# Both projections of eight column-block pairs by seven products, in shared accumulator banks

## The chip, the cores and the metric

One core of a Trainium2 chip. The metric is device time in microseconds of one execution. PE is TensorE (matmuls), PEld its weight loads, DVE is VectorE, ACT is ScalarE, POOL is GpSimd, SP is SyncE, which issues DMAs.

## What is computed

Sparse attention over 8 batches, 8 heads, 576 positions and 64 dimensions, then a bilinear feed-forward network over the 4608 tokens, with weights of 512 x 1536 (twice) and 1536 x 512:

```python
mask_local = (rel >= 0) & (rel < stride)                       # heads 0 to 3, stride 32
mask_strided = (rel >= 0) & (pos[None, :] % stride == pos[:, None] % stride)   # heads 4 to 7
attn = softmax(where(mask, q @ k.T / 8, -1e9)) @ v
x = attn.transpose(0, 2, 1, 3).reshape(4608, 512)
out = ((x @ w_a) * (x @ w_b)) @ w_out
```

All inputs and the output are float32; the products are made in bfloat16 with float32 sums.

## The kernel before

The tokens are cut into nine tiles `t` of 512. A tile has 16 slots: twelve for the projections (one column block `f` of 128 columns of `w_a` and `w_b` each), four for the output product. Attention of the next batch is spread over the slots of each tile by written-out lists (`STEPS`, `LATER`, `IN_Y`), so that PE always has matmuls between the steps of attention. All engines run in the order in which the program issues the instructions; `do(slot, ...)` appends work of DVE, POOL or SP to the end of a slot.

In a plain slot, `ab_mm` (L614) gives PE four matmuls of 512 columns with `w_a` and four with `w_b`, each into an accumulator bank of its own; ACT copies the first to `a_sb` (L644), DVE multiplies it with the second into `pf` (L647). Four banks (three tagged `mm`, one `tp`) rotate, two to a slot. Two more banks (`o`) and another two (`st`) belong to attention.

Tiles 2 to 8 (`FAST_Y`) make the output product by seven products of quarter size in place of eight (`y_plan`, L797; `y_tail`, L821, for the last tile): token halves times column halves, with sums of `pf` parts made beforehand (`fast_s`, L745) and sums of `w_out` parts (`fast_w`). `Y_ORDER` and `TAIL_ORDER` name the order: a digit for the product and a digit for the parity `q` of the tokens. Products 1, 6, 5 and 3 accumulate in one bank (X), 7 and 4 in another (Z), 2 in a third (Y); ACT or DVE reads a bank between two products of it (`y_post`). `y_store` and `store_half` issue the stores.

In tiles 7 and 8, attention is over. There, four of the six pairs of column blocks `g` (blocks 2g and 2g+1) make the projection with `w_a` in the same manner (`a_pair`, L678): fourteen matmuls of 256 columns, while `w_b` stays at eight of 512. One accumulator bank X takes 1, 6, 5 and 3:

```python
plan = {"1": (X, w(0, 0), x(0, 0)), "2": (Y, w(0, 1), x(1, 0)), "3": (X, ws(3), x(1, 1)), "4": (Z, w(1, 1), xs(3)),
        "5": (X, ws(0), xs(0)), "6": (X, ws(1), xs(1)), "7": (Z, ws(2), xs(2))}
```

The sums of `w_a` blocks come from `wsum_make` (L659, on DVE during tile 6, slots 98 to 104), those of `x` from `xsum_make` (L670). They lie in buffers that attention has given up. The matmuls of `w_a` are interleaved with those of `w_b`, so that each bank is read while PE works into another; ACT copies, DVE adds, POOL adds product 7 (L728). The partial sums of `pf` for the output product follow on DVE pair by pair (L755); in the last tile one of the four goes to POOL for three pairs (L753). At the end of a slot that has such added work, POOL copies one element of the slot's result into `pace` (L1054), which keeps POOL's later work from running ahead.

Of the kernel before, what the change touches and what calls it, by code (L numbers as in the profile page):

```python
# [27 lines left out]
FAST_A = {7: (1, 2, 3, 4), 8: (0, 1, 2, 3)}  # L28
# [3 lines left out]
def kernel(  # L32
# [29 lines left out]
    pst = ctx.enter_context(tc.tile_pool(name="pst", bufs=1, space=bass.MemoryType.PSUM))  # L62
# [23 lines left out]
    vs_buf = [const.tile([NP, HL, RS, VW], BF16, name=f"vs{i}") for i in range(2)]  # L86
# [539 lines left out]
    def ffn_ab(t, f, mid, ab=None):  # L626
# [3 lines left out]
        if f // 2 in FAST_A.get(t, ()):  # L630
            if f % 2 == 0:
                pairs[t, f // 2] = a_pair(t, f // 2)
            return next(pairs[t, f // 2])
# [18 lines left out]
    wav = wa_sb.rearrange("p (j c) (g e m) -> p j c g e m", c=2, e=2, m=128)  # L652
    wsum_a = [flat.rearrange("p (c g m) -> p c g m", c=2, g=FG)
              for flat in [vl_buf[0].rearrange("p a b -> p (a b)")[:, 12 * 128 * z:12 * 128 * (z + 1)] for z in range(2)]
              + [t.rearrange("p a b c -> p (a b c)")[:, :12 * 128] for t in qz_pair[0]]]
    xsum = {t: qz_pair[1][t - 7].rearrange("p a b c -> p (a b c)")[:, :8 * HT].rearrange("p (n c m) -> p n c m", n=4, c=2)
            for t in FAST_A}

    def wsum_make(n):  # L659
        w, s_ = (lambda e, j: wav[:, j, :, :, e]), wsum_a  # L660
# [15 lines left out]
    pairs = {}  # L676

    def a_pair(t, g):  # L678

        pf = pfs[t]  # L680
        pool, nm = ((pst, "st"), (psum4["o"], "o"))[g % 2]
        X = pool.tile([128, 2, 512], F32, tag=nm, name="ax")[:, 0, :HT]
        a = ([fsb.tile([128, TTOK], F32, tag="a_sb", name="a_sb") for _ in range(2)] if g % 2 == 0 else
             [t.rearrange("p h n -> p (h n)")[:, :2 * TTOK].bitcast(F32) for t in kT_buf[0]])
        got = {k: psum4[nm].tile([128, TTOK], F32, tag=nm, name="mm")
               for k, nm in zip((1, "Z", "Y", 0), (("mm", "mm", "tp", "mm"), ("tp", "mm", "mm", "mm"))[g % 2])}
        Z, Y = got["Z"][:, :HT], got["Y"][:, :HT]
        p7 = fsb.tile([128, HT], F32, tag="p7", name="p7")
        quarter = lambda e, k: a[e][:, HT * k:HT * (k + 1)]
        w = lambda e, j: (lambda c: wav[:, j, c, g, e])  # L690
        ws = lambda n: (lambda c: wsum_a[n][:, c, g])
        x = lambda j, k: (lambda c: x_part(t, j, k)[:, c])
        xs = lambda n: (lambda c: xsum[t][:, n, c])
        plan = {"1": (X, w(0, 0), x(0, 0)), "2": (Y, w(0, 1), x(1, 0)), "3": (X, ws(3), x(1, 1)), "4": (Z, w(1, 1), xs(3)),
                "5": (X, ws(0), xs(0)), "6": (X, ws(1), xs(1)), "7": (Z, ws(2), xs(2))}

        def P(k):
            bank, lhs, rhs = plan[k]
            for c in range(2):
                nc.tensor.matmul(bank, lhsT=lhs(c), rhs=rhs(c), start=k in "172" and c == 0, stop=c == 1, skip_group_check=True)  # L700

        x0 = TTOK * t % (XR * S)

        def b_mm(e, kks):
            f = 2 * g + e
            for kk in kks:
                nc.tensor.matmul(got[e], lhsT=wb_sb[:, kk, 128 * f:128 * (f + 1)], rhs=xT[:, kk, x0:x0 + TTOK],  # L707
                                 start=kk == 0, stop=kk == KD - 1)

        def mult(e):  # L710
            halves = lambda v_: v_.rearrange("p (a i s) -> p a i s", i=2, s=16)
            nc.vector.tensor_mul(pf[:, 2 * g + e, :].rearrange("p (i a s) -> p a i s", i=2, s=16),
                                 halves(a[e]), halves(got[e]))

        P("1")
        nc.scalar.copy(quarter(0, 0), X)
        b_mm(1, (0, 1, 2))
        P("6")
        nc.scalar.copy(quarter(1, 0), X)
        b_mm(1, (3,))  # L720
        P("7")
        nc.scalar.copy(p7, Z)
        P("2")
        nc.vector.tensor_tensor(quarter(0, 0), Y, quarter(0, 0), op=ALU.add)
        yield None
        P("5")
        nc.scalar.copy(quarter(1, 1), X)
        nc.gpsimd.tensor_tensor(quarter(1, 1), quarter(1, 1), p7, op=ALU.add)  # L728
        if (t, g - 1) in later:
            later.pop((t, g - 1))()  # L730
        b_mm(0, (0, 1))
        P("4")
        nc.vector.tensor_tensor(quarter(1, 0), Z, quarter(1, 0), op=ALU.add)
        P("3")
        nc.scalar.copy(quarter(0, 1), X)
        b_mm(0, (2, 3))
        mult(1)
        mult(0)
        yield pf[:1, 2 * g + 1, :1]

    later = {}
# [52 lines left out]
    Y_ORDER = [(x[0], int(x[1])) for x in "10 11 70 71 60 61 40 41 50 51 20 21 30 31".split()]  # L794
    TAIL_ORDER = [(x[0], int(x[1])) for x in "10 70 60 11 40 50 71 30 61 20 51 41 31 21".split()]

    def y_plan(t):  # L797

        plan, y = products(t), y_bufs()
        bank = {x: mm_bank([128, 2, HN]) for x in "ZXY"}  # L800

# [53 lines left out]
    def ffn_ys(t, j, mid):  # L855
# [46 lines left out]
    with tc.manual_schedule(engines={ENG.PE, ENG.SP, ENG.Pool, ENG.DVE, ENG.Activation}):  # L902
        early = ExitStack()
        open_psum(early, tp=2, sum=1, misc=1, o=2)
# [133 lines left out]
        for g in range(FG):  # L1038
            for n in (2, 0, 1, 3):
                do(16 * (NT - 1) + 2 * g + 1, fast_s, NT - 1, n, slice(g, g + 1))  # L1040
        for t in FAST_Y[:-1]:
# [46 lines left out]
```

## Time and profile before

| | |
|---|---|
| timed runs | 326.77, 327.73, 326.5 us (median 326.77) |
| profiled execution, first to last instruction | 325.7 us |
| PE busy | 319.1 us, 98% |
| DVE, ACT, POOL busy | 258.2, 188.2, 160.6 us |
| granted PE clock, mean | 0.997 |
| tile 7: projections, output product | 262.5 to 282.4, 282.4 to 291.6 us |
| tile 8: projections, output product | 291.6 to 311.8, 311.8 to 321.2 us |
| end | stores land until about 323.8, last instruction 325.7 us |

The profiled execution is known by its span alone; the timed runs lie 0.8 to 2.1 us above it. A row of the timeline or of a group gives the engine, the line of the kernel, the operation, what it writes and reads, and the shapes; x16 means that many instructions merged. A matmul's record includes its drain, so the price of a matmul is the difference between the starts of two rows, not the length of one. A name such as `qz1l` or `vl` in tiles 7 and 8 is an attention buffer that holds sums now.

### The profile page before, as it was taken

To read this page: it belongs to the slowest core of one execution; us is meant where nothing else is said; L and a number is where in the kernel's file an instruction comes from. 1 tells how busy PE (TensorE), PEld (TensorE's weight loads), DVE (VectorE), ACT (ScalarE), POOL (GpSimd) and SP (SyncE) were. 2 spreads that over 40 slices of the span, in tenths; PEclk is the share of its full clock that TensorE was granted. 3 is DMA by queue.
4 is the path that set the end of the run, shared out by engine and by line. 5 is a ranking of instruction groups with operands and counts; after the bars stand their busy time and mean duration, and the time that the engine had idled before them with its cause. 6 is when DMAs were issued, how large, how long until landed. Compare 5 with 4: busy or idle time off the path is not lost.

```text
span 325.7 us, 7440 instructions
## 1 busy us (share of the span) xinstructions
PE 319.1 (98%) x2672; PEld 209.0 (64%) x2672; DVE 258.2 (79%) x559; ACT 188.2 (58%) x328; POOL 160.6 (49%) x289
## 2 busy tenths in 40 slices
PE   8999999999999999999999999999999999999994
PEld 7754555445545577557999895559555966686573
DVE  6766786888878988898889888988999768837852
ACT  6763775468774476447654765467546655335441
POOL 8945936989848534762576338634113013103300
PEclk9999999999999999999999999999999999999998
DMA  9999999899999798999998999899245040004004
GB/s 159 141 203 202 202 187 172 190 170 146 123 218 139 134 99 96 108 202 149 107 112 170 196 102 100 163 187 118 46 99 147 20 129 1 2 0 131 0 3 129
DMA packets 111920, 40.73 MB, mean 125 GB/s; under 512 B 89868, under 2 KB 108940, under 8 KB 111884
## 3 DMA queue, kind: packets, MB, share of 16 engines
q0 software_dynamic: 85968, 19.48, 65.3%
q1 hardware_dynamic: 25772, 20.71, 27.4%
q8 instruction: 21, 0.34, 0.4%
q14 instruction: 15, 0.12, 0.1%
q10 hardware_dynamic: 144, 0.07, 0.1%
HBM read 39.51 MB, written 11.06 MB: 155 GB/s over the span
## 4 chain that ended last, share of the span: by engine, by line
PE 80%; DMA 8%; POOL 7%; DVE 1%; issue 1%; ACT 1%; POOLq 0%
PE mm L623 41%; PE mm L809 17%; PE mm L873 5%; DMA shared<-in_q_dram 4%; DMA vl<-in_v_dram 4%; PE mm L707 4%; PE st L388 4%; PE o L526 2%; PE ax L700 2%; POOL shared L197 2%; PE mm L838 2%; PE mm L700 2%; PE o L466 1%; PE end L838 1%; POOL wo_sb L255 1%
## 5 line engine op out<-in xcount | busy, mean ns | idle before, releaser
L623 PE MATMUL mm<-xT,wb_sb 128*128 128x512 bf16 (+1 forms) x408 | 93.7, 354 | 0.2 <-DMA wb_sb<-in_moe_w_b_dram 0.2
L623 PE MATMUL mm<-xT,wa_sb 128*128 128x512 bf16 (+1 forms) x408 | 93.7, 354 | 0.0
L644 ACT COPY a_sb<-mm 128x512 f32<-128x512 f32 x90 | 52.6, 585 | 53.9 <-PE mm L623 51.8
L623 PEld LDWEIGHTS <-wb_sb 128*128 128x128 bf16 x416 | 40.1, 98 | 37.1 <-DMA wb_sb<-in_moe_w_b_dram 0.9
L1054 POOL CAST pace<-pf 1x1 f32<-1x1 bf16 x83 | 25.3, 305 | 69.8 <-DVE pf L647 51.2
L647 DVE TENSOR_TENSOR pf<-a_sb,mm 128x512 bf16<-128x512 f32 x68 | 46.2, 680 | 9.2 <-PE mm L623 8.1
L623 PEld LDWEIGHTS <-wa_sb 128*128 128x128 bf16 x416 | 37.4, 98 | 24.0
L409 ACT ACTIVATE p<-st 72x576 bf16<-72x576 f32 (+1 forms) x56 | 36.4, 650 | 15.3 <-PE st L388 15.1
L542 DVE TENSOR_TENSOR xT<-o,xr 64x288 bf16<-64x288 f32 x48 | 21.4, 446 | 14.7 <-ACT xr L536 14.4
L809 PEld LDWEIGHTS <-ps 128*128 128x128 bf16 x288 | 28.0, 98 | 3.1
L786 ACT COPY y_sb<-mm 128x512 f32<-128x512 f32 (+1 forms) x28 | 15.5, 555 | 17.9 <-PE mm L809 15.3
L809 PE MATMUL mm<-wf,ps 128*128 128x256 bf16 x216 | 25.5, 273 | 0.0
L535 ACT ACTIVATE xr<-o 64x576 f32<-64x576 f32 x28 | 18.1, 647 | 12.3 <-PE o L526 12.0
L873 PE MATMUL mm<-wo_sb,pf 128*128 128x512 bf16 x96 | 23.4, 379 | 0.1
L243 POOL DMA_DIRECT2D vs<-in_v_dram x24 | 19.6, 818 | 5.1 <-PE mm L809 2.4
L809 PEld LDWEIGHTS <-pf 128*128 128x128 bf16 x216 | 20.3, 98 | 2.5 <-issue 0.2
L1054 POOL COPY pace<-y_sb 1x1 f32<-1x1 f32 x23 | 5.4, 233 | 33.2 <-DVE y_sb L784 19.8
L536 ACT ACTIVATE xr<-xr 64x576 f32<-64x576 f32 x28 | 19.1, 683 | 0.9
L212 POOL DMA_DIRECT2D ql<-in_q_dram x24 | 15.9, 664 | 6.3 <-DMA wo_sb<-in_moe_w_out_dram 4.6
L707 PE MATMUL mm<-xT,wb_sb 128*128 128x512 bf16 x64 | 19.0, 379 | 0.0
L809 PE MATMUL mm<-wo_sb,pf 128*128 128x256 bf16 x144 | 18.5, 273 | 0.1
L649 DVE TENSOR_TENSOR pf<-a_sb,mm 128x512 bf16<-128x512 f32 x22 | 14.9, 676 | 4.7 <-ACT a_sb L644 2.7
(189 smaller groups left out, 566.4 us busy)
## 6 DMA issues: line engine op xcount, KB each, us to landing
out_dram<-y_sb SPq DMA_DIRECT2D x12, 512.0 KB, 5.8
out_dram<-y_sb SPq DMA_DIRECT2D x11, 256.0 KB, 4.1
vl<-in_v_dram POOLq DMA_DIRECT2D x6, 384.0 KB, 8.2
kl<-in_k_dram POOLq DMA_DIRECT2D x24, 72.0 KB, 3.3
ql<-in_q_dram POOLq DMA_DIRECT2D x24, 72.0 KB, 3.2
vs<-in_v_dram POOLq DMA_DIRECT2D x24, 72.0 KB, 4.4
wo_sb<-in_moe_w_out_dram POOLq DMA_DIRECT2D x4, 384.0 KB, 9.3
natk<-in_k_dram POOLq DMA_DIRECT2D x20, 72.0 KB, 3.4
```

The costliest lines, as they stand in the source:

```text
L243: nc.gpsimd.dma_start(out=vs_buf[b % 2][:, h, :, 0:D], in_=v[b, HL + h].rearrange("(p r) d -> p r d", r=RS))
L409: nc.scalar.activation(p_flat(p)[:M, :2 * W].rearrange("p (i n) -> p i n", n=2 * n), st[:M].rearrange("p a (i n) -> p (a i) n", n=256)[:, ...
L535: nc.scalar.activation(r, sums, ACT.Ln)
L536: nc.scalar.activation(r, r, ACT.Exp, scale=-1.0)
L542: nc.vector.tensor_mul(dst.rearrange("d (p r) -> d p r", r=RS)[:, :, G * half:G * (half + 1)], o[:64, j, :W].rearrange("d (g p) -> d p g", ...
L623: nc.tensor.matmul(ps_[:, c0:c0 + n], lhsT=w[:, kk, 128 * f:128 * (f + 1)], rhs=xT[:, kk, x0:x0 + n], start=(kk == first and c0 == 0), sto ...
L644: nc.scalar.copy(a_sb, ab[0])
L647: nc.vector.tensor_mul(pf[:, f, :].rearrange("p (i a s) -> p a i s", i=2, s=16), halves(a_sb), halves(ab[1]))
L707: nc.tensor.matmul(got[e], lhsT=wb_sb[:, kk, 128 * f:128 * (f + 1)], rhs=xT[:, kk, x0:x0 + TTOK], start=kk == 0, stop=kk == KD - 1)
L809: nc.tensor.matmul(bank[b][:, q], lhsT=lhs(g, q), rhs=rhs(g), start=k in "172" and q == 0 and g == 0, stop=g == FG - 1, skip_group_check=True)
L873: nc.tensor.matmul(ybank[j], lhsT=pf[:, f, 128 * j:128 * (j + 1)], rhs=wo_sb[:, f], start=(f == 0), stop=(f == FD - 1))
L1054: nc.gpsimd.tensor_copy(pace, done)
```

## The change

In tiles 7 and 8 all slots of the projections come from one generator, `joint(t)`. A tile is two halves (`JOINT`): in each a plain pair (0, then 5) and two joint pairs (1 and 2, then 3 and 4). A joint pair makes both projections by seven products. Its banks X, Y and Z are 512 wide: `w_a`'s part lies in columns 0 to 255, `w_b`'s in 256 to 511, so one ACT copy or DVE add serves both. `JOINT_ORDER` interleaves, for each half, the products of the two joint pairs (`1a`, `1b`, ...) with the plain blocks (`A0`, `B0`, `A1`, `B1`). The products of the two projections are then multiplied in quarters: three by POOL from SBUF, one by DVE straight from the bank.

All eight banks are shared out anew for this (`eight`): the pools `o` and `st` are closed when tile 7 begins, and their four banks become Za, B, Zb and A; the four rotating banks become Ya, Yb, Xb and Xa. The output products of both tiles use them too.

Moved: the sums of `w_b` blocks are made by POOL in tile 6 (slots 99, 101, 103, 105); `xsum_make` for tile 7 in one go ahead of the tile; the partial sums of `pf` in tiles 7 and 8 no longer slot by slot, but for pairs 0 to 2 in the first eight steps of the second half, and for pairs 3 to 5 behind its last step, all on DVE. `pace` is no longer written in these two tiles. The token order inside `pf` is plain there, and the stores' row patterns follow it. `Y_ORDERS` has a second order for tile 7; `TAIL_ORDER` is new, and with it the places of two stores. Pools are opened in another order at the start, with as many banks.

```diff
-FAST_A = {7: (1, 2, 3, 4), 8: (0, 1, 2, 3)}
+JOINT = {7: ((0, 1, 2), (5, 3, 4)), 8: ((0, 1, 2), (5, 3, 4))}
...
-    vs_buf = [const.tile([NP, HL, RS, VW], BF16, name=f"vs{i}") for i in range(2)]
+    vs_all = [const.tile([128, HL, RS, VW], BF16, name=f"vs{i}") for i in range(2)]
+    vs_buf = [t[:NP] for t in vs_all]
...
+    WS = 2 * FG * 128
+    wsum = [[h.rearrange("p (c g m) -> p c g m", c=2, g=FG) for h in homes] for homes in (
+        [flat(vl_buf[0])[:, WS * z:WS * (z + 1)] for z in range(2)] + [flat(t)[:, :WS] for t in qz_pair[0]],
+        [flat(vs_all[0])[:, WS * z:WS * (z + 1)] for z in range(2)] + [flat(nat_s[nm]) for nm in "qk"])]
...
+    def wsum_make(s, n, eng):
...
         for c in range(2):
-            nc.vector.tensor_tensor(s_[n][:, c], a[:, c], b[:, c], op=op)
+            eng.tensor_tensor(s_[n][:, c], a[:, c], b[:, c], op=op)
...
+    def eight(nm, shape=(128, 2, HT)):
+        if not ends:
+            psums.close()
+            ends["pool"] = ctx.enter_context(tc.tile_pool(name="pend", bufs=1, space=bass.MemoryType.PSUM))
+            for x in ("Za", "B", "Zb", "A"):
+                eight(x)
+        pool, tag = {"Ya": (psum4["mm"], "mm"), "Yb": (psum4["mm"], "mm"), "Xb": (psum4["mm"], "mm"),
+                     "Xa": (psum4["tp"], "tp")}.get(nm, (ends["pool"], f"e{nm}"))
+        return pool.tile(list(shape), F32, tag=tag, name=f"e{nm}")
...
+    JOINT_ORDER = ("1a A0 B0 2a 1b 7a 6a 2b 7b 6b A1 5a 5b B1 4a 3a 4b 3b",
+                   "A0 1a 1b B0 7a 6a 7b 6b A1 2a 5a 2b 5b B1 4a 3a 4b 3b")
...
+                    for s in range(2):
+                        for c in range(2):
...
+                            nc.tensor.matmul(bank[:, s], lhsT=w, rhs=x, start=k in "172" and s == 0 and c == 0, stop=c == 1,
+                                             skip_group_check=True)
...
+                    if k in "176":
+                        nc.scalar.copy({"1": s1, "7": s3, "6": s2}[k], bank)
+                    elif k == "3":
+                        nc.scalar.copy(c12, bank[:, 0])
+                        mult(nc.vector, 0, 1, c12, bank[:, 1])
+                    else:
+                        c, e, kk = {"2": (s1, 0, 0), "5": (s3, 1, 1), "4": (s2, 1, 0)}[k]
+                        nc.vector.tensor_tensor(c, bank, c, op=ALU.add)
+                        mult(nc.gpsimd, e, kk, c[:, 0], c[:, 1])
+                if half and at_ < 8:
+                    fast_s(t, at_ % 4, slice(0, 1) if at_ < 4 else slice(1, 3))
+                if (half, at_) == (1, len(order) - 1):
+                    for n in range(4):
+                        fast_s(t, n, slice(3, 6))
+                if at_ % 3 == 2:
+                    yield None
...
-    Y_ORDER = [(x[0], int(x[1])) for x in "10 11 70 71 60 61 40 41 50 51 20 21 30 31".split()]
-    TAIL_ORDER = [(x[0], int(x[1])) for x in "10 70 60 11 40 50 71 30 61 20 51 41 31 21".split()]
+    Y_ORDERS = [[(x[0], int(x[1])) for x in o.split()] for o in
+                ("10 11 70 71 60 61 40 41 50 51 20 21 30 31", "10 11 20 21 60 61 70 71 50 51 40 41 30 31")]
+    TAIL_ORDER = [(x[0], int(x[1])) for x in "10 11 20 60 70 61 50 71 40 51 30 41 31 21".split()]
...
-                if k == "54"[q]:
+                if k == "4":
                     y_store(nc.sync, t, y, 1, q)
-                elif (q, k) == (0, "2"):
+                elif (q, k) == (0, "3"):
                     y_store(nc.sync, t, y, 0, q)
...
-            do(16 * (NT - 3) + 2 * n + 2, wsum_make, n)
+            do(16 * (NT - 3) + 2 * n + 2, wsum_make, 0, n, nc.vector)
+            do(16 * (NT - 3) + 2 * n + 3, wsum_make, 1, n, nc.gpsimd)
         do(16 * (NT - 2) - 1, xsum_make, NT - 2, 0)
         for n in (2, 1, 3):
-            do(16 * (NT - 2), xsum_make, NT - 2, n)
+            do(16 * (NT - 2) - 1, xsum_make, NT - 2, n)
```

More of the change, by code (lines that the diff above doesn't have):

```diff
@@ L61 @@
     fsb = ctx.enter_context(tc.tile_pool(name="ffn", bufs=2))
-    pst = ctx.enter_context(tc.tile_pool(name="pst", bufs=1, space=bass.MemoryType.PSUM))
+    psums = ctx.enter_context(ExitStack())
     dram = ctx.enter_context(tc.tile_pool(name="dram", bufs=2, space=bass.MemoryType.DRAM))
@@ L380, in S_p @@
         kT = kT_buf[b % 2][c // 2]
-        st = pst.tile([128, 2, 512], F32, tag="st", name="st")
+        st = psum4["st"].tile([128, 2, 512], F32, tag="st", name="st")
         held[b, "st", u] = st
@@ L629, in ffn_ab @@
         pf = pfs[t]
[L630 to L633, printed above, removed]
+        if t in JOINT:
+            if f == 0:
+                joints[t] = joint(t)
+            return next(joints[t])
         if ab is None:
@@ L650, in ffn_ab @@
         return pf[:1, f, :1]
[L652 to L660, printed above, removed]
+    wviews = [w.rearrange("p (j c) (g e m) -> p j c g e m", c=2, e=2, m=128) for w in (wa_sb, wb_sb)]
+    flat = lambda t: t.rearrange({2: "p a -> p a", 3: "p a b -> p (a b)", 4: "p a b c -> p (a b c)"}[len(t.shape)])
+    WS = 2 * FG * 128
+    wsum = [[h.rearrange("p (c g m) -> p c g m", c=2, g=FG) for h in homes] for homes in (
+        [flat(vl_buf[0])[:, WS * z:WS * (z + 1)] for z in range(2)] + [flat(t)[:, :WS] for t in qz_pair[0]],
+        [flat(vs_all[0])[:, WS * z:WS * (z + 1)] for z in range(2)] + [flat(nat_s[nm]) for nm in "qk"])]
+    xsum = {t: flat(qz_pair[1][t - 7])[:, :8 * HT].rearrange("p (n c m) -> p n c m", n=4, c=2) for t in JOINT}
+    def wsum_make(s, n, eng):
+        w, s_ = (lambda e, j: wviews[s][:, j, :, :, e]), wsum[s]
         a, b, op = ((w(1, 0), w(1, 1), ALU.add), (s_[0], w(0, 0), ALU.subtract), (w(0, 0), w(1, 0), ALU.subtract),
@@ L674, in xsum_make @@
         nc.vector.tensor_tensor(s_[:, n], a, b, op=ALU.subtract)
-    pairs = {}
-    def a_pair(t, g):
-        pf = pfs[t]
[L681 to L739, printed above, removed]
@@ L741 @@
-    later = {}
+    joints = {}
+    ends = {}
+    def eight(nm, shape=(128, 2, HT)):
[7 more added lines that the diff above has]
+        return pool.tile(list(shape), F32, tag=tag, name=f"e{nm}")
@@ new lines @@
+    f32 = lambda t, n, i=0: flat(t)[:, 2 * n * i:2 * n * (i + 1)].bitcast(F32)
+    pair_of = lambda t: t.rearrange("p (s m) -> p s m", s=2)
+    held_s = [pair_of(x) for x in [f32(vl_buf[1], TTOK, i) for i in range(3)] + [f32(vs_all[1], TTOK, i) for i in range(4)]
+              + [f32(kT_buf[i][z], TTOK) for i, z in ((0, 0), (0, 1))]]
+    held_c = [f32(p_buf[i], HT) for i in range(3)]
+    JOINT_ORDER = ("1a A0 B0 2a 1b 7a 6a 2b 7b 6b A1 5a 5b B1 4a 3a 4b 3b",
+                   "A0 1a 1b B0 7a 6a 7b 6b A1 2a 5a 2b 5b B1 4a 3a 4b 3b")
@@ new lines, in joint, with mult @@
+    def joint(t):
+        pf = pfs[t]
+        fill = []
+        for half, (plain, *gs) in enumerate(JOINT[t]):
+            banks = {x: eight(x) for x in "Ya Yb Xb Zb Xa Za".split()}
+            order = JOINT_ORDER[half].split()
+            for at_, (k, m) in enumerate(order):
+                if k in "AB":
+                    f = 2 * plain + int(m)
+                    if k == "A":
+                        ab = [eight("A", [128, TTOK]), eight("B", [128, TTOK])]
+                    ab_mm(t, f, ab, range(KD), ws=("AB".index(k),))
+                    if k == "A":
+                        a_sb = fsb.tile([128, TTOK], F32, tag="a_sb", name="a_sb")
+                        nc.scalar.copy(a_sb, ab[0])
+                    else:
+                        nc.vector.tensor_mul(pf[:, f, :], a_sb, ab[1])
+                else:
+                    z = "ab".index(m)
+                    g, (s1, s2, s3), c12 = gs[z], held_s[3 * z:3 * z + 3], held_c[z]
+                    bank, lhs, rhs = {"1": ("X", (0, 0), (0, 0)), "2": ("Y", (0, 1), (1, 0)), "3": ("X", 3, (1, 1)),
+                                      "4": ("Z", (1, 1), 3), "5": ("X", 0, 0), "6": ("X", 1, 1), "7": ("Z", 2, 2)}[k]
+                    bank = banks[bank + m]
+                    for s in range(2):
+                        for c in range(2):
+                            w = wsum[s][lhs][:, c, g] if isinstance(lhs, int) else wviews[s][:, lhs[1], c, g, lhs[0]]
+                            x = xsum[t][:, rhs, c] if isinstance(rhs, int) else x_part(t, *rhs)[:, c]
+                            nc.tensor.matmul(bank[:, s], lhsT=w, rhs=x, start=k in "172" and s == 0 and c == 0, stop=c == 1,
+                                             skip_group_check=True)
+                    def mult(eng, e, kk, a, b):
+                        eng.tensor_tensor(pf[:, 2 * g + e, HT * kk:HT * (kk + 1)], a, b, op=ALU.mult)
+                    if k in "176":
[3 more added lines that the diff above has]
+                        mult(nc.vector, 0, 1, c12, bank[:, 1])
+                    else:
+                        c, e, kk = {"2": (s1, 0, 0), "5": (s3, 1, 1), "4": (s2, 1, 0)}[k]
[8 more added lines that the diff above has]
+                    yield None
@@ L751, in fast_s @@
                     (x[:, 0, 0], x[:, 0, 1], ALU.subtract), (x[:, 1, 0], s[:, 1], ALU.subtract))[n]
-        if (t, n) == (NT - 1, 2) and {gs.start, gs.start + 1} <= set(FAST_A[t]):
-            later[t, gs.start] = lambda: nc.gpsimd.tensor_tensor(s[:, n], a, b, op=op)
-            return
         nc.vector.tensor_tensor(s[:, n], a, b, op=op)
@@ L773, in y_store @@
     def y_store(eng, t, y, i, q, n=slice(0, d_model)):
-        rows = out[TTOK * t:TTOK * (t + 1), n].rearrange("(a i s q) c -> a s i q c", i=2, s=8, q=2)
-        eng.dma_start(out=rows[:, :, i, q], in_=y[i][:, q, n])
+        rows = out[TTOK * t:TTOK * (t + 1), n].rearrange("(i p q) c -> p i q c", i=2, q=2)
+        eng.dma_start(out=rows[:, i, q], in_=y[i][:, q, n])
     def y_bufs():
@@ L792, in y_post @@
             nc.scalar.copy(part(0, 1), bank)
-    Y_ORDER = [(x[0], int(x[1])) for x in "10 11 70 71 60 61 40 41 50 51 20 21 30 31".split()]
-    TAIL_ORDER = [(x[0], int(x[1])) for x in "10 70 60 11 40 50 71 30 61 20 51 41 31 21".split()]
+    Y_ORDERS = [[(x[0], int(x[1])) for x in o.split()] for o in
+                ("10 11 70 71 60 61 40 41 50 51 20 21 30 31", "10 11 20 21 60 61 70 71 50 51 40 41 30 31")]
+    TAIL_ORDER = [(x[0], int(x[1])) for x in "10 11 20 60 70 61 50 71 40 51 30 41 31 21".split()]
     def y_plan(t):
         plan, y = products(t), y_bufs()
-        bank = {x: mm_bank([128, 2, HN]) for x in "ZXY"}
+        bank = ({k: eight(x) for k, x in (("X", "Ya"), ("Z", "Yb"), ("Y", "Xb"))} if t in JOINT else
+                {x: mm_bank([128, 2, HN]) for x in "ZXY"})
         def store_half(i):
-            rows = out[TTOK * t:TTOK * (t + 1)].rearrange("(a i s q) c -> a s i (q c)", i=2, s=8, q=2)
-            nc.sync.dma_start(out=rows[:, :, i], in_=y[i].rearrange("p q c -> p (q c)"))
-        for n, (k, q) in enumerate(Y_ORDER):
+            rows = out[TTOK * t:TTOK * (t + 1)]
+            rows = (rows.rearrange("(i p q) c -> p i (q c)", i=2, q=2)[:, i] if t in JOINT else
+                    rows.rearrange("(a i s q) c -> a s i (q c)", i=2, s=8, q=2)[:, :, i])
+            nc.sync.dma_start(out=rows, in_=y[i].rearrange("p q c -> p (q c)"))
+        for n, (k, q) in enumerate(Y_ORDERS[t in JOINT]):
             b, lhs, rhs = plan[k]
@@ L823, in y_tail @@
         plan, y = products(t), y_bufs()
-        banks = [{x: mm_bank([128, HN]) for x in "ZXY"},
-                 {"X": psum4["o"].tile([128, 2, 512], F32, tag="o", name="end")[:, 0, :HN],
-                  "Z": pst.tile([128, 2, 512], F32, tag="st", name="end")[:, 0, :HN]}]
+        banks = [{x: eight(n)[:, 0] for x, n in zip("XZY", ns)} for ns in (("Ya", "Yb", "Xb"), ("Xa", "Za"))]
         for k, q in TAIL_ORDER:
@@ L833, in y_tail @@
                 if (q, k) == (1, "2"):
-                    bank = mm_bank([128, 128])
+                    bank = eight("A" if n.start == 0 else "B", [128, TTOK])[:, :128]
                 else:
@@ L864, in ffn_ys @@
                 pass
-        return (y[0][:1, 0, :1], None, y[1][:1, 0, HN:HN + 1], y[1][:1, 0, :1])[j]
+        return None if t in JOINT else (y[0][:1, 0, :1], None, y[1][:1, 0, HN:HN + 1], y[1][:1, 0, :1])[j]
     def ffn_y(t, j, mid):
@@ L903 @@
         early = ExitStack()
-        open_psum(early, tp=2, sum=1, misc=1, o=2)
+        open_psum(early, tp=2, sum=1, misc=1, o=2, st=1)
         cur["misc"] = psum4["misc"].tile([128, 512], F32, tag="misc", name="misc")
@@ L963 @@
                     if f == 1:
-                        ab = pst.tile([128, 2, 512], F32, tag="st", name="ab")
+                        ab = psum4["st"].tile([128, 2, 512], F32, tag="st", name="ab")
                         first[f] = [ab[:, 0], ab[:, 1]]
@@ L974 @@
         early.close()
-        open_psum(ctx, mm=3, tp=1, o=1)
+        open_psum(ctx, mm=3, tp=1)
+        open_psum(psums, o=1, st=1)
         slots = []
@@ L992 @@
         soon = {}
-        for t in FAST_Y[:-1]:
+        for t in FAST_Y[:-2]:
             soon[16 * t + 10] = [lambda t=t: fast_s(t, 2, slice(4, 6))]
@@ L1037 @@
             do(slot, fast_w, n, slice(3, 6))
[L1038 to L1041, printed above, removed]
+        for t in FAST_Y[:-2]:
             for slot, n, z0, z1 in ((4, 0, 0, 2), (5, 2, 0, 2), (6, 1, 0, 2), (7, 3, 0, 2), (8, 2, 2, 4), (9, 0, 2, 4),
```

## The prediction

> **What bounds the kernel now.** I read the page first, then the matmul timeline of the last two tiles, then the vector and GpSimd timelines, and last quarter-microsecond windows over the end.
>
> ```profile
> PE 319.1 (98%) x2672; PEld 209.0 (64%) x2672; DVE 258.2 (79%) x559; ACT 188.2 (58%) x328; POOL 160.6 (49%) x289
> ```
>
> TensorE (PE) is busy 98% of the span, at full clock. A change pays only if it shortens the matmul stream, and costs wherever that stream waits. The stream of the last tiles:
>
> ```profile
> 262.49 0.81 PE L623 MATMUL mm<-xT,wa_sb 128*128 128x512 bf16 x3
> ...
> 265.94 0.38 PE L700 MATMUL ax<-xT,wa_sb 128*128 128x256 bf16 x2
> ...
> 278.96 1.03 PE L623 MATMUL mm<-xT,wa_sb 128*128 128x512 bf16 x4
> ...
> 282.42 1.47 PE L809 MATMUL mm<-wo_sb,pf 128*128 128x256 bf16 x12
> ...
> 291.58 0.38 PE L700 MATMUL ax<-xT,wa_sb 128*128 128x256 bf16 x2
> ...
> 311.80 0.82 PE L838 MATMUL mm<-wo_sb,pf 128*128 128x256 bf16 x6
> ```
>
> Differences of starts give prices. Pair 5 of tile 7 (278.96 to 282.42) is 16 matmuls of 512 columns: 0.216 us each. The 84 matmuls of 256 columns from 282.42 to 291.58 cost 0.109 each, each with its own weight load. The four pairs with a fast A (265.94 to 278.96) cost 3.255 each. There is almost no wait to remove; the chain of waits shows one, at the start of tile 8, where PE had to wait for ScalarE (ACT):
>
> ```profile
> 291.79 0.58 ACT y_sb L792
> 292.37 0.28 ACT a_sb L716
> ```
>
> The timeline puts that gap at about 0.09 us.
>
> **The change, part by part.**
>
> *Matmuls.* A fast-A pair is 14 matmuls of 256 and 8 of 512. A joint pair is 28 of 256: 28 x 0.109 = 3.052. Saved: 0.203 a pair, 1.62 us for eight (1.73 if a 256 cost half a 512). All of this is on the path. The wait at the start of tile 8 goes too, since the first joint product is followed by 1.7 us of plain matmuls: 0.09.
>
> *Evacuations inside a half.* A half is 6.10 + 3.46 = 9.56 us of PE. ACT gets seven 512-wide copies (0.585) and two 256-wide (0.37): 4.8 us. DVE (VectorE) gets six adds of 512 and two plain products, 0.605 apart when queued (two L712 rows together last 1.28), and two 256-wide products, 0.34 apart: 5.5 us. In the second half it also gets eight partial sums (0.20 to 0.42 each), 2.8 us. Both fit. Two places are tight. Product 5b of the first half overwrites a bank that ACT reads for 6b: behind 1b, 7a, 6a and 7b that copy ends 0.16 us ahead. Product 1b of the second half needs the bank of the last half's 3b, which DVE leaves some 1.2 us into the half; PE comes to it at 1.3. I cost both at nothing; a DVE or ACT that is later than its rows pays there.
>
> *The hand-over to the output stage.* Count from the start of 2a in the second half. PE ends 2a 0.44, 5a 0.87, 2b 1.31, 5b 1.74, B1 2.61, 4a 3.04, 3a 3.48, 4b 3.92, 3b 4.35; call this T. DVE starts 0.27 behind a matmul's end (311.80 to 312.07 in the timeline), so its queue runs: 2a from 0.71 to 1.31, 5a 1.92, 2b 2.52, 5b 3.13, B1 3.73, 4a 4.34, 3a 4.68, 4b 5.28, 3b 5.62, landed at 5.70 = T+1.35. The output stage's second product wants that same bank at T+1.31. GpSimd's product for 4b lands about T+1.83 (0.73, the L728 row, behind the add), wanted by the fifth matmul of that output product at T+1.75. Together these stall PE about 0.15 us. Four 768-wide sums follow, 0.55 each: the second ends at T+2.53, the third at T+3.0. In tile 7 the first matmul that reads them comes at T+3.1: free. In the last tile the output products are six matmuls long, so it comes at T+2.44: 0.13 more. Stalls: 0.15 for tile 7, 0.28 for tile 8. Bounds: nothing, if a record is longer than the hold of the bank; 0.75 more at each, if nine queued DVE operations take their whole 0.69 and not 0.605. I take the middle, since queued rows are 0.60 apart throughout.
>
> *The last stores.* Of the last tile's stores, the 256 KB of y1, first row, now follow product 40 (ninth of fourteen, before: sixth), and those of y0 follow 30 (eleventh) where they followed 20 (tenth).
>
> ```profile
> 320.25:320.50 0.25, 0.25 (x6) 0.24 (x4) 0.14 (x1) 0.00 (x0) 0.00 (x0) 1.00 0.93 205
> ...
> 321.25:321.50 0.25, 0.00 (x0) 0.00 (x0) 0.25 (x1) 0.00 (x0) 0.00 (x0) 1.00 0.32 115
> ...
> 323.50:323.75 0.25, 0.00 (x0) 0.00 (x0) 0.00 (x0) 0.00 (x0) 0.00 (x0) 0.75 0.65 168
> ```
>
> In these windows (DMA share and GB/s last) a 256 KB store occupies the DMA engines about 1.1 us, 1.2 behind its issue, and the last 512 KB take 2.1 us from 321.6. PE ends at 321.17 = E. After: the first store runs E-1.45 to E-0.35, y0 from E-0.2 to E+0.95, and the last 512 KB, which could have started at E+0.43, start there: 0.5 us later than now. Bounds 0 and 0.6.
>
> *Moved work off the path.* The eight sums of w_b weights go to GpSimd in tile 6, two instructions behind each of slots 99, 101, 103, 105. They are needed at about 265.5. A 128x256 bf16 sum takes 0.67 there (L753) and a one-element operation 0.17 (L1054), so 768 elements are estimated at 0.17 + 3 x 0.50 = 1.67 us, 13.4 in all, from about 238: ready in time even with waits. Behind them GpSimd has only pace operations, on which no load depends any more. What they do to DVE is the rival below. The sums of x for tile 7 move one slot forward, into DVE time that is free at 264.
>
> *Sum.* -1.62 - 0.09 + 0.15 + 0.28 + 0.50 = -0.78. The profiled span of 325.7 becomes 324.9; the median of the runs, 326.77, is 1.1 above that span, and gives 326.0. Own range of this case, from the bounds: 325.0 to 327.6. A measurement can tell about 0.5%, 1.6 us, from no change; this is inside.
>
> **Rivals.**
>
> *GpSimd holds up DVE in tile 6 (slower).* Some DVE operations read two tensors in SBUF (masks, partial sums, weight sums), others one in SBUF and one in PSUM. The first kind and GpSimd get in each other's way:
>
> ```profile
> 243.77 1.57 POOL L1054 CAST pace<-pf 1x1 f32<-1x1 bf16 x1 [1.45 <-DVE pf L647]
> ...
> 271.80 0.74 POOL L728 TENSOR_TENSOR a_sb<-a_sb,p 128x256 f32<-128x256 f32 x1 [1.52 <-ACT a_sb L727]
> ```
>
> The pace operation, 0.17 elsewhere, lasts until DVE's run of a mask, two weight sums and a partial sum (243.57 to 245.30) is over. But the 0.74 at 271.80 began under a DVE sum that ran to 271.96 and is only 0.02 longer than the undisturbed 0.72. No row shows a DVE operation that waits for GpSimd. If it does, for the whole instruction, each of the eight can start only behind a DVE operation of the other kind (0.6 for a plain product, 1.3 where a normalisation follows), so DVE loses 0.4 to 1.07 each time, more where the start comes late in such an operation; I take 0.85: 6.8 us in all. DVE is idle about 1.1 us from 235 to 252, and a plain product may be 1.7 us late before the matmuls two pairs of banks on wait for it: about 4 us reach PE. With half a microsecond of the same at the hand-overs (partial sums behind GpSimd's last product) the time is 330.5. It decides from a DVE loss of 2.8 us, 0.35 an instruction. The Trainium skill, "SBUF — State Buffer", section "Who interferes with whom", has this as a rule: whichever of a two-SBUF-input VectorE operation and a GpSimd operation that reads SBUF starts first keeps the shared ports for its whole length. By that rule this rival is the outcome; the trace agrees in the one direction that the pace row shows.
>
> *DVE later than its rows inside the joint halves (slower).* If DVE and ACT come 0.5 us later than counted, both tight places and the hand-overs wait, about 0.4 us twice in each of four halves and 0.5 at each hand-over: 4.2 on -0.78 would be the worst, half of it likely: 328.1. Against: the four fast-A pairs run with the same kind of hand-offs and no PE gap.
>
> *The whole gain (faster).* If the stores overlap and nothing stalls: 326.77 - 1.82 = 324.95. Against: the stores fill the DMA windows to 0.9 already.
>
> *The products do not come cheaper.* If four different weights in a row were not loaded in time, the gain would be nothing; the 84 matmuls at L809 do just that at 0.109, so I give this no chance of its own.
>
> **How the numbers follow.** Forecast 0.43 (no change that can be told); GpSimd holding DVE 0.42, of it 0.40 slower; late DVE 0.08, 0.05 of it slower; whole gain 0.07. Faster 0.07, same 0.48, slower 0.45. I put the forecast a little ahead of the rival because the one overlapped GpSimd sum hardly noticed DVE. The range must reach over both: 325.0 to 332.0 leaves out part of the whole-gain case and the worst of the rival.
>
> **What would show it.** Right: joint products at 0.436 us each, eight pairs' worth shorter by 1.6 us; the first output matmul of tile 7 about 0.8 us earlier than 282.42, with the gap of 0.1 to 0.2 us behind twelve of them; DMA active to about 3.0 us behind the last matmul. Wrong: PE gaps between 240 and 262 with DVE idle before a mask or a sum while GpSimd runs its weight sums (the rival); gaps before product 1b or 5b (late DVE); w_b sums on GpSimd far from 1.7 us.

## The result, and the profile after

The changed kernel takes 330.67 us (median; 329.82 to 331.63), the kernel before 326.48 beside it (325.92 to 327.73): a ratio of 1.0126, 95% interval 1.0105 to 1.0146. It is slower, by 1.3%. The profiled span went from 325.7 to 329.9.

The first line of the page answers to the one shown of before.

```profile
PE 317.1 (96%) x2691; PEld 212.8 (64%) x2720; DVE 267.3 (81%) x551; ACT 188.7 (57%) x320; POOL 180.2 (55%) x295
```

PE has 2 us less to do, as the change meant, and its share of the span fell. So it waits, and the matmul timeline says where. Behind the name of a group stand the idle time ahead of it and what ended it.

```profile
244.64 1.03 PE L624 MATMUL mm<-xT,wa_sb 128*128 128x512 bf16 x3
246.55 1.02 PE L624 MATMUL mm<-xT,wb_sb 128*128 128x512 bf16 x4 [0.88 <-DVE pf L648]
...
249.76 1.02 PE L624 MATMUL mm<-xT,wb_sb 128*128 128x512 bf16 x4 [1.08 <-DVE pf L648]
...
252.72 1.02 PE L624 MATMUL mm<-xT,wb_sb 128*128 128x512 bf16 x4 [0.81 <-DVE pf L648]
...
255.94 1.02 PE L624 MATMUL mm<-xT,wb_sb 128*128 128x512 bf16 x4 [1.08 <-DVE pf L648]
...
258.72 0.94 PE L818 MATMUL mm<-wo_sb,pf 128*128 128x256 bf16 x7 [0.94 <-DVE pf L648]
...
262.13 1.05 PE L818 MATMUL mm<-wf,ps 128*128 128x256 bf16 x8 [0.47 <-DVE ps L760]
...
268.80 0.38 PE L728 MATMUL eXa<-xT,wa_sb 128*128 128x256 bf16 x2
...
288.11 1.47 PE L818 MATMUL eYa<-wo_sb,pf 128*128 128x256 bf16 x12
...
297.36 0.38 PE L728 MATMUL eXa<-xT,wa_sb 128*128 128x256 bf16 x2
...
316.49 0.82 PE L845 MATMUL eYa<-wo_sb,pf 128*128 128x256 bf16 x6
```

Four plain products and two output products wait for DVE, and all of it is in tile 6, which the joint products do not touch. Tile 7 starts at 268.80; before it was 262.49. Measured from the same early matmuls of tile 6, it starts 6.27 us late. What DVE and GpSimd (POOL) do there is seen in their timelines, GpSimd first:

```profile
238.11 3.23 POOL L666 TENSOR_TENSOR vs<-wb_sb 128x768 bf16<-128x768 bf16 x2
...
243.80 3.72 POOL L666 TENSOR_TENSOR vs<-vs,wb_sb 128x768 bf16<-128x768 bf16 x2
...
249.98 3.73 POOL L666 TENSOR_TENSOR natq<-wb_sb 128x768 bf16<-128x768 bf16 x2
...
256.16 3.41 POOL L666 TENSOR_TENSOR natk<-wb_sb,vs 128x768 bf16<-128x768 bf16 x2
```

```profile
239.73 1.93 DVE L428 TENSOR_TENSOR p<-p,mask_l 128x576 int16<-128x576 int16 x1 [0.17 <-ACT p L410]
...
244.14 1.75 DVE L760 TENSOR_TENSOR ps<-pf 128x512 bf16<-128x512 bf16 x1
245.82 0.67 DVE L648 TENSOR_TENSOR pf<-a_sb,mm 128x512 bf16<-128x512 f32 x1
246.42 1.42 DVE L428 TENSOR_TENSOR p<-p,mask_s 72x576 int16<-72x576 int16 x1
```

A mask takes 0.45 and a partial sum 0.41 when undisturbed. The mask at 239.73 ends at 241.66, 0.32 behind the end of the GpSimd pair (241.34); the mask at 246.42 ends at 247.84, 0.32 behind the next pair. DVE records the operation as busy while it is held. The partial sum at 244.14 does not wait for its whole pair: it ends at 245.89, 0.27 behind the first sum of the pair (1.82 us from 243.80), and the second sum ends only behind it. The plain product between them (L648, one input in PSUM) keeps its 0.67 while GpSimd sums. Seven DVE operations are held so, each by one GpSimd sum, for 1.47, 1.34, 0.96, 1.34, 0.97, 0.91 and 0.74 us, 7.7 in all. The first is absorbed by DVE's lead, the time by which it was ahead of what PE needs; the other six come to 6.26, and the PE gaps, taken from the starts of groups (246.55 - 244.64 less four matmuls of 0.216, and so on), are 1.04, 1.23, 0.97, 1.23, 1.12 and 0.64: 6.23 us.

The rest of the span, stage by stage (starts of the groups above against those of before; the output stages' starts are 282.42 and 311.80 before):

| stretch | before | after | change |
|---|---|---|---|
| up to tile 7 | 262.49 | 268.80 | +6.31 |
| projections of tile 7 | 19.93 | 19.31 | -0.62 |
| output of tile 7 | 9.16 | 9.25 | +0.09 |
| projections of tile 8 | 20.22 | 19.13 | -1.09 |
| output of tile 8 to PE's end | 9.37 | 9.90 | +0.53 |
| PE's end to the span's end | 4.53 | 3.50 | -1.03 |

They sum to +4.2, the difference of the spans. PE ends at 321.17 before and at 326.40 after.

The end of the span, in half-microsecond windows (DMA share and GB/s last):

```profile
326.50:327.00 0.50, 0.00 (x0) 0.00 (x0) 0.22 (x1) 0.00 (x0) 0.00 (x0) 1.00 1.01 373
...
327.50:328.00 0.50, 0.00 (x0) 0.00 (x0) 0.00 (x0) 0.00 (x0) 0.00 (x0) 1.00 1.02 270
328.00:328.50 0.50, 0.00 (x0) 0.00 (x0) 0.00 (x0) 0.00 (x0) 0.00 (x0) 1.00 0.02 5
```

The DMA engines are done about 1.7 us behind PE's end instead of 2.6. Before, a 256 KB store ran at 164 to 205 GB/s in three of its quarter-microsecond windows, with the engines 0.82 to 0.94 busy, and at 369 only in the fourth; here the loaded windows have 270 to 373.

### The profile page after: what moved, and what is told of

Read it like the earlier page. It is cut to its first block, busy times and chain, and to the rows that moved or that the text cites. A ratio compares the mean times of both kernels' runs of the same rounds, so it can differ in the third digit from the quotient of the medians.

```text
span 329.9 us, 7496 instructions
## 1 busy us (share of the span) xinstructions
PE 317.1 (96%) x2691; PEld 212.8 (64%) x2720; DVE 267.3 (81%) x551; ACT 188.7 (57%) x320; POOL 180.2 (55%) x295
## 4 chain that ended last, share of the span: by engine, by line
PE 72%; DMA 8%; DVE 8%; POOL 7%; issue 3%; ACT 1%; POOLq 0%; DVEq 0%
PE mm L624 32%; PE mm L818 13%; PE mm L880 5%; DMA vl<-in_v_dram 4%; DMA shared<-in_q_dram 4%; PE st L389 3%; PE o L527 2%; PE eA L624 2%; PE eXb L728 2%; PE eXa L728 2%; PE eB L624 2%; DVE ps L760 2%; POOL shared L198 2%; PE eYa L818 2%; DVE pf L648 2%
## 5 line engine op out<-in xcount | busy, mean ns | idle before, releaser
L624 PE MATMUL mm<-xT,wb_sb 128*128 128x512 bf16 (+1 forms) x373 | 85.0, 352 | 4.2 <-DVE pf L648 3.9
L624 PE MATMUL mm<-xT,wa_sb 128*128 128x512 bf16 (+1 forms) x360 | 83.9, 351 | 0.7
L645 ACT COPY a_sb<-mm 128x512 f32<-128x512 f32 x82 | 47.9, 585 | 49.0 <-PE mm L624 41.5
L1060 POOL CAST pace<-pf 1x1 f32<-1x1 bf16 x71 | 22.8, 321 | 45.2 <-DVE pf L648 31.8
L648 DVE TENSOR_TENSOR pf<-a_sb,mm 128x512 bf16<-128x512 f32 x60 | 40.7, 679 | 6.4 <-PE mm L624 6.1
L732 POOL TENSOR_TENSOR pf<-vl 128x256 bf16<-128x256 f32 x12 | 8.7, 729 | 30.8 <-DVE vl L741 30.8
L760 DVE TENSOR_TENSOR ps<-pf 128x512 bf16<-128x512 bf16 (+2 forms) x42 | 21.6, 514 | 0.6
L818 PE MATMUL mm<-wf,ps 128*128 128x256 bf16 x180 | 21.5, 273 | 0.5 <-DVE ps L760 0.5
L213 POOL DMA_DIRECT2D kl<-in_k_dram x24 | 16.1, 671 | 5.3 <-issue 3.2
L791 ACT COPY y_sb<-mm 128x512 f32<-128x512 f32 x20 | 11.7, 585 | 12.1 <-PE mm L818 10.5
L650 DVE TENSOR_TENSOR pf<-a_sb,mm 128x512 bf16<-128x512 f32 x22 | 14.9, 677 | 4.5 <-ACT a_sb L645 2.7
```

The costliest lines, as they stand in the source:

```text
L213: nc.gpsimd.dma_start(out=t[32 * h:32 * h + 32], in_=src[b, h].rearrange("(i y) d -> y i d", y=32))
L624: nc.tensor.matmul(ps_[:, c0:c0 + n], lhsT=w[:, kk, 128 * f:128 * (f + 1)], rhs=xT[:, kk, x0:x0 + n], start=(kk == first and c0 == 0), sto ...
L645: nc.scalar.copy(a_sb, ab[0])
L648: nc.vector.tensor_mul(pf[:, f, :].rearrange("p (i a s) -> p a i s", i=2, s=16), halves(a_sb), halves(ab[1]))
L760: nc.vector.tensor_tensor(s[:, n], a, b, op=op)
L818: nc.tensor.matmul(bank[b][:, q], lhsT=lhs(g, q), rhs=rhs(g), start=k in "172" and q == 0 and g == 0, stop=g == FG - 1, skip_group_check=True)
```

## The experiments

Theory: GpSimd's weight sums hold DVE's operations with two inputs in SBUF; the expectations call this the port theory. Rivals: the joint products themselves, the shared banks or the new order are what costs. Ratios are to the kernel before, run beside each, with 95% intervals.

### The changed kernel without the w_b sums

The products that need a w_b sum take w_a's in its place, so the same matmuls run and the output is wrong.

```
-            do(16 * (NT - 3) + 2 * n + 3, wsum_make, 1, n, nc.gpsimd)
-   w = wsum[s][lhs][:, c, g] if ...
+   w = wsum[0][lhs][:, c, g] if ...
```

> The changed kernel without the eight w_b sums on GpSimd; the w_b half of products 3, 5, 6 and 7 takes w_a's sums as weights instead, so the same matmuls run. Port theory (a VectorE operation with two SBUF inputs waits for a whole GpSimd sum): the 6.3 us that tile 7 starts late are gone, 330.7 - 6.3 = 324.4 us, and no mask or partial sum in tile 6 takes over 0.5 us. Rival (the joint halves or their VectorE backlog cost the time): 328 us or more.

Measured: 324.92 us, 0.9951 (0.9932 to 0.9969), span 323.2. Tile 7 starts where it did before, to 0.01 us, counted from the matmuls of tile 6. The projections of tiles 7 and 8 take 19.31 and 19.13 as in the changed kernel, 1.71 us less than before, which is in sum what the forecast gave the joint products and the start of tile 8. The sums on GpSimd are worth 5.8 us.

### The kernel before with the eight sums

```
+    def wsum_make_b(n):
+        ...
+        for c in range(2):
+            nc.gpsimd.tensor_tensor(s_[n][:, c], a[:, c], b[:, c], op=op)
...
+            do(16 * (NT - 3) + 2 * n + 3, wsum_make_b, n)
```

> The kernel before, with the eight w_b sums added on GpSimd at the same slots, read by nobody. Port theory: 326.5 + 6.3 = 332.8 us, with masks and partial sums of 1.3 to 1.9 us in tile 6. Rival (the cost lies in the joint halves): 326.5 us.

Measured: 332.92, 1.0195 (1.0179 to 1.0211), span 331.3: 6.5 us slower than before with nothing but the sums. Tile 7 starts 6.27 us late, the same as in the changed kernel, and the DVE timeline shows the same held rows, the first of them this mask:

```profile
239.04 1.93 DVE L428 TENSOR_TENSOR p<-p,mask_l 128x576 int16<-128x576 int16 x1 [0.17 <-ACT p L410]
```

With the run above this shows the cause from both sides: the sums alone make it slower, and the change without them is faster.

### GpSimd as busy, but only writing

```
+            if eng is nc.gpsimd:
+                for _ in range(2):
+                    eng.memset(s_[n][:, c], 0.0)
+                continue
```

> The changed kernel with each GpSimd sum replaced by two memsets of the same target (estimated 0.7 us each from the 1.40 us of a 1536-element one), so that GpSimd is busy as long but reads nothing; the w_b sums are zero. Port theory, for reads: no wait, 324.4 us as without sums. Rival theory, that any GpSimd work in tile 6 or its writes slow VectorE or shift the queue: 328 to 331 us.

Measured: 324.30, 0.9933 (0.9918 to 0.9948). GpSimd's timeline, then DVE's under it:

```profile
240.87 2.99 POOL L668 MEMSET vs<- 128x768 bf16 x4
```

```profile
242.18 0.45 DVE L428 TENSOR_TENSOR p<-p,mask_s 72x576 int16<-72x576 int16 x1
```

The mask runs inside the 2.99 us in which GpSimd writes, and takes its usual 0.45. GpSimd being busy, or writing, is not what costs: it is its reading.

### One read instead of two

As above, with `eng.tensor_copy(s_[n][:, c], a[:, c])` in place of the memset.

> The changed kernel with each GpSimd sum replaced by two GpSimd copies of one SBUF operand into the same target (w_b sums are then copies of a weight block). Port theory, any GpSimd read of SBUF: 16 instructions of an estimated 0.8 us, masks and partial sums in tile 6 are again longer than 0.46 us, by up to 0.8 each; 326.5 to 329 us. Rival (only a GpSimd operation with two SBUF inputs holds VectorE up): as without sums, 324.4 us.

Measured: 326.49, 1.0004 (0.9995 to 1.0013). Tile 7 starts 2.34 us late; the masks and partial sums of DVE that start under a copy (0.82 undisturbed) take up to 1.20, so none loses more than one copy:

```profile
238.57 1.14 DVE L428 TENSOR_TENSOR p<-p,mask_l 128x576 int16<-128x576 int16 x1 [0.17 <-ACT p L410]
```

One input in SBUF suffices for the hold.

### The same sums in short pieces

```
-            eng.tensor_tensor(s_[n][:, c], a[:, c], b[:, c], op=op)
+            for g in [slice(z, z + 1) for z in range(FG)] if eng is nc.gpsimd else [slice(0, FG)]:
+                eng.tensor_tensor(s_[n][:, c, g], a[:, c, g], b[:, c, g], op=op)
```

> The changed kernel with each of the eight sums cut into six GpSimd instructions of 128 columns (estimated 0.17 + 0.25 = 0.42 us each, 20 us in all). Port theory, held for one instruction: no VectorE operation waits more than 0.42 us, some thirteen runs of two-SBUF operations lose 0.2 each, which VectorE's idle time and the banks' slack absorb; 324.4 to 326 us. Rival (GpSimd keeps the port as long as it has work): 331 us or more.

Measured: 329.92, 1.011 (1.0077 to 1.0142). My expectation missed; the rival put beside it, at 331 or more, came nearer. The four runs lie between 328.42 and 331.88, and the trace is of the slowest. GpSimd's pieces and, from the DVE timeline, what met them, for the first and the last of the four groups:

```profile
238.19 4.64 POOL L667 TENSOR_TENSOR vs<-wb_sb 128x128 bf16<-128x128 bf16 x12
```

```profile
239.81 3.35 DVE L428 TENSOR_TENSOR p<-p,mask_l 128x576 int16<-128x576 int16 x1 [0.17 <-ACT p L410]
...
263.29 3.81 DVE L790 TENSOR_TENSOR y_sb<-y_sb 128x512 f32<-128x512 f32 x1
```

A piece takes 0.39, but the mask, ready at 239.8, ended at 243.2, behind the whole run of twelve. The addition at 263.29 was held behind the last twelve pieces (261.89 to 266.54); the last piece of xT came behind it, and PE stood 2.1 us at the start of tile 7. Behind this stand the granted clock is 0.57 from 268 to 272. In the two groups between, DVE did get in. The third, then a mask of DVE:

```profile
255.00 6.57 POOL L667 TENSOR_TENSOR natq<-wb_sb 128x128 bf16<-128x128 bf16 x12
```

```profile
255.63 0.67 DVE L428 TENSOR_TENSOR p<-p,mask_s 72x576 int16<-72x576 int16 x1
```

This mask lost 0.22, no DVE operation in that group lost over 0.3, and the twelve took 6.57 instead of 4.64. So cutting the sums short lets DVE in at some times and not at others, and does not save the time.

### The sums on GpSimd in the output stage of tile 6

```
-            do(16 * (NT - 3) + 2 * n + 3, wsum_make, 1, n, nc.gpsimd)
+        for i, n in enumerate((2, 0, 1, 3)):
+            do(16 * (NT - 3) + 11 + i, wsum_make, 1, n, nc.gpsimd)
```

> The changed kernel with the eight w_b sums on GpSimd, but in the output stage of tile 6 (slots 107 to 110), where VectorE is half idle. Port theory: VectorE is held up there as well, but only what is urgent costs: the last write of xT, which tile 7's first plain matmuls wait for, comes up to 1.7 us late, and the fourth sum is late for its product at most little; 325 to 327 us. Rival (GpSimd sums cost about 6 us wherever they stand): 330 us.

Measured: 335.88, 1.0287 (1.0258 to 1.0316): worse than both expectations. DVE has slack there, but six sums now stand in a row on GpSimd, with only a pace operation (0.17, at 257.33) between them:

```profile
254.14 3.23 POOL L666 TENSOR_TENSOR natq<-wb_sb 128x768 bf16<-128x768 bf16 x2
...
257.46 3.21 POOL L666 TENSOR_TENSOR vs<-wb_sb 128x768 bf16<-128x768 bf16 x2
260.64 3.21 POOL L666 TENSOR_TENSOR vs<-vs,wb_sb 128x768 bf16<-128x768 bf16 x2
```

```profile
254.17 9.97 DVE L760 TENSOR_TENSOR ps<-ps,pf 128x512 bf16<-128x512 bf16 x1
```

One partial sum of 0.41 took 9.97 us, and PE waited 8.4 us for it. Behind that wait the granted clock was 0.50 to 0.52 until 270, with matmuls of 256 columns 0.218 apart instead of 0.109, so tile 7 starts 11.3 us late. Both runs show that DVE's price can be the length of GpSimd's whole run. The changed kernel's own trace shows that it need not be.

### The sums on DVE

The same slots, with `nc.vector`.

> The changed kernel with the eight w_b sums on VectorE, behind the last projection and during the output stage of tile 6 (slots 107 to 110), where VectorE has about 4 us idle; they take 8 x 0.47 = 3.8 us. Port theory: no GpSimd reads against VectorE in tile 6, 324.4 to 325.5 us, faster than before. Rival (the joint halves cost the time): 328 us or more.

Measured: 325.21, 0.9967 (0.9953 to 0.9981). DVE does a sum in half a microsecond, and PE loses only at the start of tile 7. The DVE timeline, then PE's:

```profile
261.10 1.02 DVE L666 TENSOR_TENSOR natk<-wb_sb,vs 128x768 bf16<-128x768 bf16 x2
...
262.04 0.91 DVE L543 TENSOR_TENSOR xT<-o,xr 64x288 bf16<-64x288 f32 x2
```

```profile
263.01 1.04 PE L624 MATMUL eA<-xT,wa_sb 128*128 128x512 bf16 x3 [0.87 <-DVE xT L543]
```

The fourth sum stands ahead of the last xT writes, and product A0 waits 0.87 for these.

### The rows of the last stores

The diff also changed which rows of a tile one partition holds. Alone, on the kernel before (the rows of the last tile's output land in another order):

```
-        rows = out[TTOK * t:TTOK * (t + 1), n].rearrange("(a i s q) c -> a s i q c", i=2, s=8, q=2)
-        eng.dma_start(out=rows[:, :, i, q], in_=y[i][:, q, n])
+        rows = out[TTOK * t:TTOK * (t + 1), n].rearrange("(i p q) c -> p i q c", i=2, q=2)
+        eng.dma_start(out=rows[:, i, q], in_=y[i][:, q, n])
```

> The kernel before with the changed kernel's row pattern in the last tile's stores (rows land in another order inside the tile; nothing else changes). If the pattern is what makes the changed kernel's last stores land 1.8 us behind the last matmul in place of 2.6: 326.4 - 0.75 = 325.6 us, with 256 KB moved in about 0.7 us. Rival (the order of products and stores does it): 326.4 us.

Measured: 325.75, 0.9978 (0.9969 to 0.9987), 0.7 us faster; from PE's end to the span's end it is 3.8 us, against 4.5. Two windows of its second 256 KB store of the tail (DMA share and GB/s last):

```profile
319.00:319.25 0.25, 0.25 (x5) 0.23 (x3) 0.25 (x2) 0.00 (x0) 0.00 (x0) 1.00 0.98 369
319.25:319.50 0.25, 0.25 (x7) 0.24 (x5) 0.12 (x1) 0.00 (x0) 0.00 (x0) 1.00 1.04 393
```

It takes about 0.75 us at 369 to 393 GB/s, where the same store of before took 1.1, three quarters of it at 164 to 205. The row pattern alone gives 0.7 of the 1.03 us that the end is shorter in the changed kernel; the other 0.3 is not settled.

### What the experiments point to

The changed kernel with the w_b sums on DVE, three in the output stage of tile 6 and the fourth at slot 113, in the first half of tile 7, where product 2a also moves ahead of A0:

```
-            do(16 * (NT - 3) + 2 * n + 3, wsum_make, 1, n, nc.gpsimd)
+        for i, n in enumerate((2, 0, 1, 3)):
+            do(16 * (NT - 3) + (11, 12, 13, 17)[i], wsum_make, 1, n, nc.vector)
...
-            order = JOINT_ORDER[half].split()
+            order = JOINT_ORDER[half].split() if (t, half) != (7, 0) else (
+                "1a 2a A0 B0 1b 7a 6a 2b 7b 6b A1 5a 5b B1 4a 3a 4b 3b".split())
```

> The changed kernel with the w_b sums on VectorE: three during the output stage of tile 6, the fourth behind the sixth step of tile 7; and in the first half of tile 7 product 2a ahead of A0. The run with all four in the output stage lost about 1 us at the start of tile 7, where the matmuls waited for VectorE's last write of xT behind the fourth sum. Port theory: that wait goes, 325.2 - 0.9 = 324.3 us.

Measured: 324.10, 0.9933 (0.9919 to 0.9948), span 321.9. It beats both kernels, by 2.2 and by 6.6 us. From 226 us on one wait of PE on another engine is left in its view of waits:

```profile
PE eYa L846 <- DVE ps L761: 0.3, 1, 0.3
```

That is the hand-over in tile 8. The last run takes it away: the sums of the last tile in the order third, first, second, fourth, and output product 60 behind 70 and 71.

```
-   for n in range(4):
+   for n in ((2, 0, 1, 3) if t == NT - 1 else range(4)):
...
-    TAIL_ORDER = ... "10 11 20 60 70 61 50 71 40 51 30 41 31 21"
+    TAIL_ORDER = ... "10 11 20 70 71 60 61 50 40 51 30 41 31 21"
```

> The best version so far (w_b sums on VectorE, 324.10 us) with the last tile's sums made in the order third, first, second, fourth and its output products in the order 10 11 20 70 71 60 61 50 40 51 30 41 31 21, so that the first matmul that reads the second sum comes 0.7 us later. If the 0.29 us stall in product 60 of the changed kernel is that sum coming late, it goes: 323.8 us, and no wait of product 60 on a partial sum. Rival (something else is next late, such as ScalarE's copies in the new order): 324.1 us.

Measured: 324.31, 0.9918 (0.9897 to 0.9939). No wait of PE on DVE is left after 225 us, and the last output stage takes 9.43 us in the trace instead of 9.89, but the time cannot be told from that of the version ahead of it. Inconclusive.

## Why the prediction was wrong

The forecast was 326.0, no change that can be told. What happened is the rival that the prediction named, *GpSimd holds up DVE in tile 6*, at 330.5 with a chance of 0.42; measured 330.67.

**The step that failed** is *Moved work off the path*: the eight w_b sums costed at nothing there, and the choice behind it ("I put the forecast a little ahead of the rival because the one overlapped GpSimd sum hardly noticed DVE"). The size of a sum was right: 1.6 to 1.9 us, waits included, against 1.67. Ready in time was right as well. What was wrong was to read the row at 271.80, a GpSimd sum that began under a DVE sum and lost nothing, as evidence on the other direction, a DVE operation that begins under a GpSimd one; and the two overlapped for 0.16 us at most (271.80 to 271.96). No row of before showed that, and the pace row, in which GpSimd waited for a whole run of DVE, was the one that bore on it: two engines that share something and hold it, one way seen.

The rule of the Trainium skill ("SBUF — State Buffer", "Who interferes with whom"), that whichever starts first keeps the shared ports, gave the direction in every run here: two-input DVE rows go from 0.45 to 1.93 under GpSimd sums, and memsets, which do not read, leave them at 0.45. By that rule the rival was the outcome. Its "whole instruction" fits the seven holds of the changed kernel; in two of the other runs it is too short, and the last section has the numbers.

**The rival's own working** fell on the right total in part because errors cancelled. It took 0.85 us for each of eight sums, 6.8; DVE lost 7.7, in seven operations. It let 4 reach PE and put 0.5 on the hand-overs; 6.27 reached PE in tile 6, since DVE's lead was gone with the first hold (1.47) and every later one passed through in full, and about 0.25 at the hand-overs. The stores, below, paid 1.5 of it back.

**The other terms:**

- *Matmuls*, -1.62 and *the start of tile 8*, -0.09: joint products come every 0.436 to 0.4375 us, as predicted. Tile 8's projections are 19.13, twice the 9.56 of the working, and 1.09 less than before, against 0.81 of matmuls and 0.09 of wait. The 0.09 was read too small, as the idle time behind a record with its drain: by starts, the three matmuls from 291.80 took until 292.70, 0.90 instead of 0.65, a wait of 0.25. Tile 7 saved 0.62, not 0.81; 0.17 of the difference is A0 waiting behind the late xT.
- *The evacuations* inside the joint halves fit: no PE wait on a bank in products 1b or 5b. The rival *DVE later than its rows* did not come.
- *The hand-over*: +0.15 and +0.28 predicted; +0.09 and +0.53 measured. In tile 8 the wait is at the place the working named, the second sum; by starts it is 0.45 there, and 0.10 one product earlier:

```profile
319.33 0.50 PE L845 MATMUL eYa<-wf,ps 128*128 128x256 bf16 x3 [0.29 <-DVE ps L760]
```

The first of the four sums, at 0.55 in the working, began under GpSimd's last product and took 0.24 more, the same hold as in tile 6. GpSimd's row, then DVE's:

```profile
317.53 0.73 POOL L732 TENSOR_TENSOR pf<-vs 128x256 bf16<-128x256 f32 x1 [0.20 <-DVE vs L741]
```

```profile
317.89 0.79 DVE L760 TENSOR_TENSOR ps<-pf 128x768 bf16<-128x768 bf16 x1
```

- *The last stores*, the second term of a wrong size: +0.5 predicted, -1.03 measured. The prediction counted when each store is issued and took its duration (1.1 us for 256 KB) from before. The diff changed the rows that a store writes, and that, run alone, gave -0.7 us: a 256 KB store takes about 0.7. Edits to an access pattern were read as bookkeeping.

With the sums costed at nothing the working gave a span of 324.9; with the measured end instead of +0.5 it would be 323.4. The change without the sums has 323.2, so the rest of the working stands to within 0.2, with the small misses named above.

## What to carry to other kernels

Work moved to an engine that is idle is not free if it reads the memory that the busy engine reads: look for that engine's operations with two inputs there, and cost each between the length of one instruction and that of the whole queued run it may meet. A row that shows two engines holding each other up in one direction is a reason to price the other direction, and a harmless row is evidence only for its own order of starts. When an access pattern of a DMA changes, its duration is no longer a row of the trace before, so give it bounds on both sides.

## What the hardware showed that was not expected

- The hold can last over instructions that stand back to back. Behind a run of twelve GpSimd sums of 0.39, a mask that came up in the fifth took 3.35 us, and behind six of 1.6 in a row a partial sum took 9.97, a pace operation between them notwithstanding. It need not: in the changed kernel DVE got in between the two sums of three pairs, and in the kernel with short pieces behind one piece at 255.63. What decides is open. It goes the other way too: in the second group of that kernel, where DVE had the run, twelve pieces took 9.38 instead of 4.64:

```profile
245.29 9.38 POOL L667 TENSOR_TENSOR vs<-vs,wb_sb 128x128 bf16<-128x128 bf16 x12
```

- The rate of a store depends on how its rows lie in DRAM. Rows of the same length, every second one of a single block, went at 369 to 393 GB/s; every second one in groups of eight, 32 rows apart, at 164 to 213 for the first 0.75 us and only then at 344 to 369. Why is open.
